# 32 products of zeros on TensorE around the first sums and transposes of a gated recurrence with a mixture of adapters

## The chip, the cores and the metric

The kernel runs on one core of one Trainium2 chip. The metric is the device time of one execution in microseconds, and the kernel before was timed in three runs. A profile of one execution by the hardware profiler goes with it. All times below that carry a place in the execution count from the start of the profile's span.

## The reference

Two steps follow each other. The first is a gated linear recurrence over 768 time steps, for each of 4 batches and 8 heads with a head size of 48:

```python
for t in range(S):
    state = alpha[:, :, t, :, None] * state + np.einsum('bhd,bhe->bhde', k[:, :, t], v[:, :, t])
    y[:, :, t] = np.einsum('bhd,bhde->bhe', q[:, :, t], state)
```

The result, laid out as 3072 rows of 384, goes through a mixture of adapters: each row chooses two of eight adapters by the largest of `x @ w_gate`, weighs them with a softmax over the two, and adds `w * (x @ A[e]) @ B[e]` (rank 16) to itself:

```python
w = np.exp(sel)
w /= w.sum(-1, keepdims=True) + 1e-09
delta[mask] += w[mask, k, None] * (z @ B[e])
return (x + delta).astype(np.float32)
```

Inputs and output are float32: 19 MB to read, 4.7 MB to write.

## The kernel before

**Units.** The work is cut into 24 units: 4 batches of 6 chunks of 128 time steps, with all 8 heads of a chunk in one unit. Within a chunk the recurrence is written as products; from chunk to chunk a state of 48x48 per head is carried. For unit u the steps are:

- `ln` (ScalarE): logarithm of alpha, for one or two units at a time.
- `cum` (TensorE, L249 to L253): sums of the logarithms over the time steps of the chunk, one product with a triangular matrix, one small one with the identity and four of two columns.
- `exp` (ScalarE): the exponential of the sums and of their negative.
- `ka`, `kg` (GpSimd, L265): k and q times these, into `kgq`. In some units k and q go in two instructions (`ka` then `kg`), in the others in one (`kg`).
- `tr` (TensorE, L285) and `kq` (ScalarE): eight 128x128 transposes into a bank of PSUM, and its copy to SBUF (`kt`).
- `at` (TensorE, L298): eight products, of keys with queries, into `at_t`. This tile takes up two banks and exists once.
- `msk` (VectorE, L302): `at_t` times a triangular mask, to SBUF. `at` of the next unit waits for it, as it writes the same tile.
- `vb` (GpSimd, L279), `kv` (TensorE), `st` (VectorE, L308): cast of v, the state's update, and its scaling.
- `av` (TensorE) and `ysb` (ScalarE): the unit's output, copied into `o_t`.
- `xb` (GpSimd, L347, half of the units), `xt` (TensorE, L356), `xs` (ScalarE): the output transposed for the adapters.

For groups of up to three units the adapters follow: `z` (products with the adapters and the gate together), `gm`, `df`, `ge`, `gx`, `wu`, `dn`, `w` (choice and weights, VectorE, one exponential on ScalarE), `zw`, `zt`, `zs` (weighting and transposing). Then for each unit `dl` (TensorE, L450) and `o` (VectorE, L457) add the adapters' part, and `out` stores the unit.

**Order.** Nothing is scheduled by a planner. One list, `ORDER`, gives every step in the order in which it is issued: `cum.7.4` is step `cum` of unit 7 into bank 4 of the five free banks `M_t`. Each engine executes its own instructions in this order, and waits for the semaphores of what it needs. `Sa.12.6` in the list is a load: queue S (SP) or A (ScalarE), tensor a, k, q or v, first unit, number of units. So a load from ScalarE is issued when ScalarE's program comes to it, behind its activations. Weights have the letter w.

**Loads.** Eight loads stand ahead of everything: alpha and q of batch 0, part of the weights and alpha of batch 1 from SP, k of batch 0 and the rest of the weights from ScalarE. The others follow inside the list. Each of the four inputs has two buffers, for even and odd batches. Written out by names with the first unit of the batch, the order in which their bytes come is: a0, k0, q0, v0, weights, a6, k6, q6, v6, a12, k12, q12, v12, a18, k18, q18, v18. All stores wait for the last of these.

**Around the change.** The first steps on TensorE are `cum.0` and `cum.1`, then `cum.2`, `cum.5` and `cum.3`, then `tr.0`, whose first four transposes need only k and whose last four need q, then `cum.4`, `tr.1` and `at.0`. Constants are set ahead of the list: VectorE clears padding in `lg` (L179) and `kgq` (L187), GpSimd builds the triangular matrix and the identity.

Of the kernel before, what the change touches and what calls it, by code (L numbers as in the profile page):

```python
# [39 lines left out]
ORDER = """  # L40
Sa.0.6 Aw.3.0 Sq.0.6 Aw.2.0 Sw.0.0 Ak.0.6 Sw.1.0 Sa.6.6 ln.0 Sq.6.6 ln.1 cum.0.0 cum.1.1 ln.4 exp.0 ln.2 exp.1
cum.2.2 Sa.12.6 ka.0 cum.5.3 Av.0.6 cum.3.4 exp.2 ka.1 exp.3 ka.2 kg.0 kg.1 tr.0.0 cum.4.1 kq.0 ka.3 tr.1.2 exp.5
at.0 kg.2 kq.1 msk.0 exp.4 kg.3 tr.2.4 cw.0 at.1 kg.4 msk.1 tr.3.0 Ak.6.6 kq.2 vb.0 kq.3 at.2 vb.1 kv.0 ka.4 av.0.3
st.1 ysb.0 msk.2 kv.1 vb.2 av.1.2 xb.0 tr.4.1 ysb.1 kg.5 st.2 at.3 xt.0.4 msk.3 ln.8 av.2.0 ka.5 Sq.12.6 kv.2 ln.6
st.3 vb.5 tr.5.3 xs.0 vb.4 ysb.2 cum.6.2 kq.4 cum.7.4 vb.3 kq.5 xb.2 at.4 exp.6 kv.3 msk.4 xt.2.0 xt.1.1 exp.7 ka.6
cum.9.3 st.4 cum.8.2 Av.6.6 xs.2 at.5 ln.10 ka.7 kv.4 msk.5 xs.1 Sa.18.6 exp.8 z.0.4 av.3.0 kg.6 exp.9 gm.0 av.4.1
st.5 ysb.3 kg.7 tr.6.2 ge.0 ysb.4 df.0 gx.0 av.5.3 kq.6 wu.0 kg.8 xt.3.0 dn.0 ysb.5 w.0 tr.7.1 xs.3 zw.0 at.6 kq.7
xt.5.2 msk.6 cum.11.3 xb.4 xs.5 zt.0.0 kg.9 xt.4.4 cum.10.1 xs.4 at.7 Ak.12.6 exp.10 tr.8.2 msk.7 z.1.4 zs.0 kq.8
vb.6 tr.9.1 gm.1 vb.7 exp.11 kv.6 at.8 kg.10 df.1 st.7 gx.1 av.6.0 msk.8 ln.12 av.7.2 kv.7 kq.9 cum.12.3 vb.8 st.8
ysb.6 dl.0.1 at.9 kg.11 ge.1 ysb.7 o.0 tr.10.0 ln.14 msk.9 av.8.2 kq.10 dl.2.1 kv.8 ysb.8 vb.9 dl.1.0 o.2 Sq.18.6  # L50
at.10 exp.12 vb.11 wu.1 cum.13.2 st.9 xt.7.1 xb.8 exp.13 dn.1 o.1 kv.9 xb.6 w.1 tr.11.3 Av.12.6 vb.10 xs.7 zw.1
cum.14.0 kq.11 ka.12 xt.8.2 msk.10 xt.6.1 zt.1.4 xs.8 cum.15.3 xs.6 zs.1 av.9.2 ka.13 exp.14 st.10 dl.3.1 z.2.4 o.3
ysb.9 kg.12 at.11 ln.16 gm.2 kv.10 msk.11 dl.4.0 kg.14 exp.15 tr.12.2 xt.9.1 kq.12 df.2 av.10.3 st.11 xs.9 cum.16.2
ge.2 o.4 gx.2 ysb.10 at.12 kg.13 wu.2 exp.16 tr.14.1 msk.12 dl.5.0 xb.10 kq.14 tr.13.3 kg.15 av.11.2 dn.2 o.5 kq.13
cum.17.1 w.2 Ak.18.6 xt.10.0 ysb.11 at.13 zw.2 xs.10 xt.11.3 msk.13 vb.12 tr.15.2 xs.11 vb.13 kv.12 exp.17 z.3.0
kg.16 st.13 at.14 ln.18 gm.3 av.13.4 msk.14 zt.2.3 kq.15 kv.13 cum.18.1 kg.17 zs.2 ysb.13 av.12.2 df.3 ge.3 st.14
at.15 ysb.12 tr.16.3 msk.15 exp.18 dl.7.4 vb.14 gx.3 tr.17.2 kq.16 wu.3 vb.15 o.7 kv.14 ln.20 vb.16 av.14.1 dn.3
st.15 xb.12 at.16 ysb.14 w.3 cum.19.3 vb.17 msk.16 kq.17 av.15.4 xb.14 Av.18.6 out.2 xt.13.1 exp.19 ka.18 out.7
kv.15 zw.3 xt.14.2 xs.13 at.17 st.16 xs.14 ka.19 xt.12.3 ysb.15 msk.17 zt.3.0 dl.6.1 xs.12 cum.20.2 ln.22 z.4.4
kg.18 o.6 zs.3 dl.8.3 exp.20 kv.16 gm.4 kg.19 tr.18.0 o.8 xt.15.1 kq.18 df.4 st.17 out.8 kg.20 dl.9.2 cum.21.3 xs.15  # L60
out.3 o.9 dl.10.0 gx.4 at.18 exp.21 out.5 o.10 tr.19.1 ge.4 msk.18 out.10 cum.22.2 kq.19 kg.21 av.17.0 out.6 exp.22
dl.11.3 av.16.1 wu.4 o.11 at.19 ysb.17 out.0 dn.4 tr.20.2 msk.19 ysb.16 out.9 vb.18 tr.21.3 kq.20 out.11 xb.16 kv.18
out.4 xt.17.0 kq.21 vb.19 w.4 st.19 at.20 out.1 vb.20 xs.17 xt.16.1 zw.4 cum.23.2 kg.22 xs.16 kv.19 msk.20 exp.23
z.5.3 st.20 at.21 kg.23 gm.5 av.18.0 tr.22.4 msk.21 ysb.18 kv.20 kq.22 av.20.1 ge.5 vb.21 df.5 at.22 st.21 gx.5
ysb.20 av.19.2 vb.22 wu.5 msk.22 zt.4.0 xb.18 ysb.19 kv.21 vb.23 tr.23.4 zs.4 dn.5 xb.20 dl.14.1 st.22 xt.19.2 kq.23
w.5 kv.22 xs.19 o.14 at.23 zw.5 xt.18.0 out.14 xt.20.4 msk.23 av.22.2 xs.18 xs.20 dl.12.1 z.6.3 ysb.22 o.12 xb.22
av.21.0 zt.5.4 gm.6 ysb.21 xt.22.2 dl.13.1 st.23 zs.5 xt.21.0 xs.22 df.6 ge.6 o.13 gx.6 dl.15.4 dl.17.2 xs.21 wu.6
o.15 av.23.1 z.7.0 dn.6 o.17 out.15 ysb.23 dl.16.4 out.13 gm.7 xt.23.2 w.6 out.17 df.7 ge.7 zw.6 gx.7 xs.23 wu.7
o.16 z.8.3 zt.6.2 gm.8 dn.7 out.16 zs.6 df.8 w.7 gx.8 out.12 dl.19.4 wu.8 dl.18.2 zw.7 o.18 zt.7.0 o.19 zs.7 dl.20.2
out.18 dl.21.0 w.8 o.20 dl.22.4 out.19 zw.8 out.20 o.21 zt.8.2 o.22 zs.8 out.21 dl.23 out.22 o.23 out.23  # L70
"""


# [18 lines left out]
def kernel(  # L92
# [43 lines left out]
    def act(*args, **kw):  # L136
        recent[:] = [nc.scalar.activation(*args, **kw)]  # L137
# [11 lines left out]
    def load(ring, x, u, n, *name):  # L149
        eng = dict(S=nc.sync, A=nc.scalar)[ring]  # L150
        if x == "w":
            eng.dma_start(out=WSRC[u][0], in_=WSRC[u][1])
            return
        b, c = _place(u)
        if n == NCH:
            dma = eng.dma_start(out=home(x, b)[:, :, 0:D],  # L156
                                in_=SRC[x][b].rearrange("h (c j) d -> j (h c) d", j=C))
# [82 lines left out]
    def ln(u):  # L240
        i, _ = lof[u]
        n = len(LNS[i])
        b, c = _place(u)
        act(lgs[i % KEEP["lg"]][:, 0:n, :, 0:D],
            chunks(home("a", b))[:, c:c + n, :, 0:D], AF.Ln)

    def cum(u):
# [1 line left out]
        nc.tensor.matmul(r[:, 0:DM], suf[:, :], t[:, :, 0:D], start=True, stop=True)  # L249
        nc.tensor.matmul(r[:, DM:DM + 2 * NP], ident[:, :], off.rearrange("p a b -> p (a b)"),  # L250
                         start=True, stop=False, skip_group_check=True)
        for p in range(NP):
            nc.tensor.matmul(r[:, DM + 2 * p:DM + 2 * p + 2], pair(t, p), ones[:, :],  # L253
                             start=False, stop=(p == NP - 1), skip_group_check=True)
# [257 lines left out]
```

## Time and profile before

| | |
|---|---|
| median of 3 runs | 95.35 us (94.91 to 95.42) |
| the profiled execution itself | 95.33 us |
| its span, first to last instruction | 93.4 us |
| TensorE products, busy | 69.4 us (74%), 1088 |
| VectorE, busy | 62.8 us (67%), 165 |
| ScalarE, busy | 64.9 us (70%), 164 |
| GpSimd, busy | 62.6 us (67%), 82 |
| loads and stores | 24.17 MB, mean 259 GB/s |

In the profile PE is TensorE with its products, PEld its loading of weights, DVE is VectorE, ACT ScalarE, POOL GpSimd and SP SyncE; a q behind a name (ACTq) is the engine's queue, which issues loads. A line of a timeline gives start and length in us, engine, line of the code, operation, output and inputs, shape and count; in brackets stands how long the engine had been idle before and what ended the wait. The chain of waits gives start, length and the piece of work. A line of the busy times by stretches gives the stretch, its length, for each of PE, PEld, DVE, ACT and POOL the busy time (and the number of instructions), then the granted clock of TensorE, the busy share of the DMA engines and GB/s. Products on TensorE are pipelined: one of 128 columns is listed with its whole length, though the next starts before it ends.

### The profile page before, as it was taken

How to read it: one execution, taken by the hardware profiler on the slowest of the kernel's cores; microseconds unless marked ns; L12 is line 12 of the kernel's file. 1: busy time of each engine (PE TensorE's matmuls, PEld its weight loads, DVE VectorE, ACT ScalarE, POOL GpSimd, SP SyncE). 2: the span in 40 equal slices, each digit the busy share in tenths (PEclk: the TensorE clock that was granted, in tenths of full speed). 3: DMA queues.
4: the chain of work that ended last, by engine and by line, in shares of the span. 5: the costliest groups of instructions: out<-in, count | busy, mean ns of one | idle time of the engine just before them, and what ended most of it. 6: DMA issues, size and time to landing. Idle time of an engine off the chain costs nothing.

```text
span 93.4 us, 2795 instructions
## 1 busy us (share of the span) xinstructions
PE 69.4 (74%) x1088; PEld 54.7 (59%) x1088; DVE 62.8 (67%) x165; ACT 64.9 (70%) x164; POOL 62.6 (67%) x82
## 2 busy tenths in 40 slices
PE   0004080988899999959999998999999989994510
PEld 0002050756778697847788886887687878861100
DVE  5000000054954969796999999799999999999920
ACT  5004990794389999769999966999899666744120
POOL 6000087999793899998769999987999994200000
PEclk9999999999999999999999999999999999999965
DMA  1999999999999599999989999999817791216681
GB/s 18 292 315 317 316 316 316 301 316 303 316 313 269 163 307 305 291 310 313 307 223 316 313 294 303 305 307 286 253 68 278 263 381 51 84 49 252 259 305 66
DMA packets 29645, 24.17 MB, mean 259 GB/s; under 512 B 1856, under 2 KB 29632, under 8 KB 29632
## 3 DMA queue, kind: packets, MB, share of 16 engines
q1 hardware_dynamic: 16928, 14.35, 49.6%
q10 hardware_dynamic: 12704, 9.65, 36.3%
q8 instruction: 8, 0.13, 0.6%
q14 instruction: 5, 0.04, 0.2%
HBM read 19.28 MB, written 4.72 MB: 257 GB/s over the span
## 4 chain that ended last, share of the span: by engine, by line
DMA 32%; DVE 25%; PE 14%; ACT 12%; POOL 5%; issue 5%; SPq 2%; ACTq 2%; DVEq 0%; POOLq 0%
DMA a_t<-in_alpha_dram 18%; DMA kq_t<-in_q_dram 14%; DVE am L302 11%; DVE o_t L457 5%; POOL kgq L265 4%; ACT ex L137 4%; PE M_t L285 3%; PE at_t L298 3%; DVE sb L308 3%; ACT o_t L140 2%; DVE zw L433 2%; ACT kt L140 2%; SPq L156 2%; ACTq L156 2%; PE M_t L450 1%
## 5 line engine op out<-in xcount | busy, mean ns | idle before, releaser
L265 POOL TENSOR_TENSOR kgq<-kq_t,ex 128x384 bf16<-128x384 f32 (+1 forms) x36 | 45.0, 1274 | 12.9 <-DMA kq_t<-in_k_dram 9.7
L302 DVE TENSOR_TENSOR am<-at_t,mask 128x1024 bf16<-128x1024 f32 x24 | 29.3, 1219 | 20.7 <-PE at_t L298 20.6
L137 ACT ACTIVATE ex<-M_t 128x392 f32<-128x392 f32 (+1 forms) x48 | 21.6, 534 | 0.6 <-PE at_t L298 0.5
L285 PE MATMUL M_t<-ident,kgq 128*128 128x128 bf16 x192 | 17.3, 238 | 2.8 <-POOL kgq L265 2.7
L140 ACT COPY kt<-M_t 128x512 f32<-128x512 f32 x24 | 14.7, 615 | 4.5 <-PE M_t L285 3.9
L249 PE MATMUL M_t<-lg,suf 128*128 128x384 bf16 x24 | 8.6, 366 | 12.1 <-ACT lg L137 12.1
L140 ACT COPY o_t<-M_t 128x384 f32<-128x384 f32 x25 | 12.4, 520 | 5.7 <-PE M_t L339 5.0
L137 ACT ACTIVATE lg<-a_t 128x768 bf16<-128x768 f32 (+1 forms) x13 | 10.5, 824 | 7.9 <-DMA a_t<-in_alpha_dram 7.1
L285 PEld LDWEIGHTS <-kgq 128*128 128x128 bf16 x192 | 12.8, 105 | 5.0 <-POOL kgq L265 3.4
L457 DVE TENSOR_TENSOR o_t<-M_t,o_t 128x384 f32<-128x384 f32 x23 | 12.4, 549 | 1.2 <-PE M_t L450 1.1
L308 DVE TENSOR_TENSOR sb<-S_t,ex 128x384 bf16<-128x384 f32 x20 | 11.0, 549 | 1.7 <-PE S_t L322 1.7
L279 POOL CAST vb<-v_t 128x384 bf16<-128x384 f32 x24 | 11.6, 506 | 0.0
L298 PE MATMUL at_t<-kt 48*128 48x128 bf16 x192 | 10.4, 233 | 1.3 <-DVE am L302 0.9
L339 PE MATMUL M_t<-vb,am 128*128 128x48 bf16 x192 | 9.2, 188 | 0.0
L347 POOL CAST xb<-o_t 128x384 bf16<-128x384 f32 x12 | 6.0, 505 | 4.6 <-ACT o_t L140 4.6
L250 PEld LDWEIGHTS <-ident 128*128 128x128 bf16 x24 | 2.4, 101 | 11.1 <-issue 10.8
L298 PEld LDWEIGHTS <-kt 48*128 48x128 bf16 x192 | 6.3, 99 | 4.0 <-issue 2.1
L450 PE MATMUL M_t<-B_all,zs 128*128 128x384 bf16 x24 | 7.3, 327 | 1.0 <-ACT zs L140 0.8
L339 PEld LDWEIGHTS <-am 128*128 128x128 bf16 x192 | 7.5, 100 | 0.3
L322 PE MATMUL S_t<-vb,kgq 128*128 128x96 bf16 x80 | 7.1, 216 | 0.0
L332 PE MATMUL M_t<-sb,kt 128*128 128x96 bf16 x80 | 7.1, 213 | 0.1
L356 PE MATMUL M_t<-ident,o_t 128*128 128x128 f32 x36 | 7.0, 303 | 0.2 <-DVE o_t L457 0.2
(53 smaller groups left out, 101.6 us busy)
## 6 DMA issues: line engine op xcount, KB each, us to landing
out_dram<-o_t SPq DMA_DIRECT2D x24, 192.0 KB, 2.3
B_st<-in_moe_B_dram ACTq DMA_DIRECT2D x1, 192.0 KB, 2.7
W_st<-in_moe_A_dram SPq DMA_DIRECT2D x2, 96.0 KB, 9.4
a_t<-in_alpha_dram SPq DMA_DIRECT2D x4, 0.2 KB, 12.9
kq_t<-in_q_dram SPq DMA_DIRECT2D x4, 0.2 KB, 16.6
kq_t<-in_k_dram ACTq DMA_DIRECT2D x4, 0.2 KB, 8.7
v_t<-in_v_dram ACTq DMA_DIRECT2D x4, 0.2 KB, 7.5
G_st<-in_moe_w_gate_dram ACTq DMA_DIRECT2D x1, 12.0 KB, 5.5
```

The lines of the kernel that those rows point to most:

```text
L137: recent[:] = [nc.scalar.activation(*args, **kw)]
L140: recent[:] = [nc.scalar.copy(*args)]
L249: nc.tensor.matmul(r[:, 0:DM], suf[:, :], t[:, :, 0:D], start=True, stop=True)
L265: nc.gpsimd.tensor_tensor(out=kgq[u % KEEP["kg"]][:, part, :, 0:D], in0=kq_t[b % 2].rearrange("p w (h c) d -> p w c h d", c=NCH)[:, part, ...
L279: nc.gpsimd.tensor_copy(out=vbt[u % KEEP["vb"]], in_=chunks(home("v", b))[:, c, :, 0:D])
L285: nc.tensor.transpose(t[:, w, p, :], pair(kgq[u % KEEP["kg"]][:, w], p), ident[:, :])
L298: nc.tensor.matmul(at_t[:, hh, p, :], kq[rows, 0, p, :], kq[rows, 1, p, :], start=True, stop=True)
L302: nc.vector.tensor_tensor(out=am[u % KEEP["am"]].rearrange("p a b t -> p (a b) t"), in0=at_t.rearrange("p a b t -> p (a b) t"), in1=_bc_mi ...
L308: nc.vector.tensor_tensor(out=sb[u % KEEP["sb"]].rearrange("p a b d -> p (a b) d"), in0=S_t.rearrange("p a b d -> p (a b) d"), in1=_bc(ex[ ...
L339: nc.tensor.matmul(y[:, h * D:(h + 1) * D], am[u % KEEP["am"]][:, hh, p, :], vbt[u % KEEP["vb"]][:, h, :], start=(c == 0 and h == 0), stop ...
L450: nc.tensor.matmul(bank("av" if hold else "dl", u)[:, 0:DM], zst[g % KEEP["zs"]].bitcast(F2)[:, j * P:(j + 1) * P], B_all[:, :], start=not ...
L457: nc.vector.tensor_tensor(out=o_t[u], in0=bank("dl", u)[:, 0:DM], in1=o_t[u], op=ALU.add)
```

## The change

A tile of 128x512 zeros in bfloat16 is set on VectorE ahead of the other constants. A new step `busy.N` issues N products of a 128x128 part of it with all 512 columns of it, into the first half of `at_t`. Nothing reads these results; the first `at` writes the tile anew, on the same engine. Four such steps stand in the list, with 13, 10, 7 and 2 products: ahead of `cum.0`, between `cum.1` and `cum.2`, between `cum.3` and `tr.0`, and between `tr.1` and `at.0`. The rest of the list has the same steps in the same order, with its lines broken in other places; the steps of the gates and the unit that is kept in PSUM (`HOLD`) are the same in both kernels.

```diff
 ORDER = """
-Sa.0.6 Aw.3.0 Sq.0.6 Aw.2.0 Sw.0.0 Ak.0.6 Sw.1.0 Sa.6.6 ln.0 Sq.6.6 ln.1 cum.0.0 cum.1.1 ln.4 exp.0 ln.2 exp.1
-cum.2.2 Sa.12.6 ka.0 cum.5.3 Av.0.6 cum.3.4 exp.2 ka.1 exp.3 ka.2 kg.0 kg.1 tr.0.0 cum.4.1 kq.0 ka.3 tr.1.2 exp.5
-at.0 kg.2 kq.1 msk.0 exp.4 kg.3 tr.2.4 cw.0 at.1 kg.4 msk.1 tr.3.0 Ak.6.6 kq.2 vb.0 kq.3 at.2 vb.1 kv.0 ka.4 av.0.3
+Sa.0.6 Aw.3.0 Sq.0.6 Aw.2.0 Sw.0.0 Ak.0.6 Sw.1.0 Sa.6.6 ln.0 Sq.6.6 ln.1 busy.13 cum.0.0 cum.1.1 ln.4 exp.0 ln.2 exp.1
+busy.10 cum.2.2 Sa.12.6 ka.0 cum.5.3 Av.0.6 cum.3.4 exp.2 ka.1 exp.3 ka.2 kg.0 kg.1 busy.7 tr.0.0 cum.4.1 kq.0 ka.3
+tr.1.2 exp.5 busy.2 at.0 kg.2 kq.1 msk.0 exp.4 kg.3 tr.2.4 cw.0 at.1 kg.4 msk.1 tr.3.0 Ak.6.6 kq.2 vb.0 kq.3 at.2 vb.1
...
+    zero = consts.tile([P, 512], F2, name="zero")
+    nc.vector.memset(zero, 0.0)
     suf = consts.tile([P, P], F2, name="suf")
...
+    def busy(n):
+
+        for _ in range(n):
+            nc.tensor.matmul(at_t[:, 0].rearrange("p a s -> p (a s)"), zero[:, 0:P], zero[:, :],
+                             start=True, stop=True)
+
...
-               w=w, zw=zw, zt=zt, zs=zs, dl=dl, o=o, out=store, cw=cw)
+               w=w, zw=zw, zt=zt, zs=zs, dl=dl, o=o, out=store, cw=cw, busy=busy)
```

More of the change, by code (lines that the diff above doesn't have):

```diff
@@ L40 @@
 ORDER = """
-Sa.0.6 Aw.3.0 Sq.0.6 Aw.2.0 Sw.0.0 Ak.0.6 Sw.1.0 Sa.6.6 ln.0 Sq.6.6 ln.1 cum.0.0 cum.1.1 ln.4 exp.0 ln.2 exp.1
-cum.2.2 Sa.12.6 ka.0 cum.5.3 Av.0.6 cum.3.4 exp.2 ka.1 exp.3 ka.2 kg.0 kg.1 tr.0.0 cum.4.1 kq.0 ka.3 tr.1.2 exp.5
-at.0 kg.2 kq.1 msk.0 exp.4 kg.3 tr.2.4 cw.0 at.1 kg.4 msk.1 tr.3.0 Ak.6.6 kq.2 vb.0 kq.3 at.2 vb.1 kv.0 ka.4 av.0.3
-st.1 ysb.0 msk.2 kv.1 vb.2 av.1.2 xb.0 tr.4.1 ysb.1 kg.5 st.2 at.3 xt.0.4 msk.3 ln.8 av.2.0 ka.5 Sq.12.6 kv.2 ln.6
-st.3 vb.5 tr.5.3 xs.0 vb.4 ysb.2 cum.6.2 kq.4 cum.7.4 vb.3 kq.5 xb.2 at.4 exp.6 kv.3 msk.4 xt.2.0 xt.1.1 exp.7 ka.6
@@ L46 @@
[L46 to L55, printed above, removed]
@@ L56 @@
-kg.16 st.13 at.14 ln.18 gm.3 av.13.4 msk.14 zt.2.3 kq.15 kv.13 cum.18.1 kg.17 zs.2 ysb.13 av.12.2 df.3 ge.3 st.14
[L57 to L70, printed above, removed]
+Sa.0.6 Aw.3.0 Sq.0.6 Aw.2.0 Sw.0.0 Ak.0.6 Sw.1.0 Sa.6.6 ln.0 Sq.6.6 ln.1 busy.13 cum.0.0 cum.1.1 ln.4 exp.0 ln.2 exp.1
@@ new lines @@
+busy.10 cum.2.2 Sa.12.6 ka.0 cum.5.3 Av.0.6 cum.3.4 exp.2 ka.1 exp.3 ka.2 kg.0 kg.1 busy.7 tr.0.0 cum.4.1 kq.0 ka.3
+tr.1.2 exp.5 busy.2 at.0 kg.2 kq.1 msk.0 exp.4 kg.3 tr.2.4 cw.0 at.1 kg.4 msk.1 tr.3.0 Ak.6.6 kq.2 vb.0 kq.3 at.2 vb.1
+kv.0 ka.4 av.0.3 st.1 ysb.0 msk.2 kv.1 vb.2 av.1.2 xb.0 tr.4.1 ysb.1 kg.5 st.2 at.3 xt.0.4 msk.3 ln.8 av.2.0 ka.5
+Sq.12.6 kv.2 ln.6 st.3 vb.5 tr.5.3 xs.0 vb.4 ysb.2 cum.6.2 kq.4 cum.7.4 vb.3 kq.5 xb.2 at.4 exp.6 kv.3 msk.4 xt.2.0
+xt.1.1 exp.7 ka.6 cum.9.3 st.4 cum.8.2 Av.6.6 xs.2 at.5 ln.10 ka.7 kv.4 msk.5 xs.1 Sa.18.6 exp.8 z.0.4 av.3.0 kg.6
@@ new lines @@
+exp.9 gm.0 av.4.1 st.5 ysb.3 kg.7 tr.6.2 ge.0 ysb.4 df.0 gx.0 av.5.3 kq.6 wu.0 kg.8 xt.3.0 dn.0 ysb.5 w.0 tr.7.1 xs.3
+zw.0 at.6 kq.7 xt.5.2 msk.6 cum.11.3 xb.4 xs.5 zt.0.0 kg.9 xt.4.4 cum.10.1 xs.4 at.7 Ak.12.6 exp.10 tr.8.2 msk.7 z.1.4
+zs.0 kq.8 vb.6 tr.9.1 gm.1 vb.7 exp.11 kv.6 at.8 kg.10 df.1 st.7 gx.1 av.6.0 msk.8 ln.12 av.7.2 kv.7 kq.9 cum.12.3
+vb.8 st.8 ysb.6 dl.0.1 at.9 kg.11 ge.1 ysb.7 o.0 tr.10.0 ln.14 msk.9 av.8.2 kq.10 dl.2.1 kv.8 ysb.8 vb.9 dl.1.0 o.2
+Sq.18.6 at.10 exp.12 vb.11 wu.1 cum.13.2 st.9 xt.7.1 xb.8 exp.13 dn.1 o.1 kv.9 xb.6 w.1 tr.11.3 Av.12.6 vb.10 xs.7
@@ new lines @@
+zw.1 cum.14.0 kq.11 ka.12 xt.8.2 msk.10 xt.6.1 zt.1.4 xs.8 cum.15.3 xs.6 zs.1 av.9.2 ka.13 exp.14 st.10 dl.3.1 z.2.4
+o.3 ysb.9 kg.12 at.11 ln.16 gm.2 kv.10 msk.11 dl.4.0 kg.14 exp.15 tr.12.2 xt.9.1 kq.12 df.2 av.10.3 st.11 xs.9
+cum.16.2 ge.2 o.4 gx.2 ysb.10 at.12 kg.13 wu.2 exp.16 tr.14.1 msk.12 dl.5.0 xb.10 kq.14 tr.13.3 kg.15 av.11.2 dn.2 o.5
+kq.13 cum.17.1 w.2 Ak.18.6 xt.10.0 ysb.11 at.13 zw.2 xs.10 xt.11.3 msk.13 vb.12 tr.15.2 xs.11 vb.13 kv.12 exp.17 z.3.0
+kg.16 st.13 at.14 ln.18 gm.3 av.13.4 msk.14 zt.2.3 kq.15 kv.13 cum.18.1 kg.17 zs.2 ysb.13 av.12.2 df.3 ge.3 st.14
@@ new lines @@
+at.15 ysb.12 tr.16.3 msk.15 exp.18 dl.7.4 vb.14 gx.3 tr.17.2 kq.16 wu.3 vb.15 o.7 kv.14 ln.20 vb.16 av.14.1 dn.3 st.15
+xb.12 at.16 ysb.14 w.3 cum.19.3 vb.17 msk.16 kq.17 av.15.4 xb.14 Av.18.6 out.2 xt.13.1 exp.19 ka.18 out.7 kv.15 zw.3
+xt.14.2 xs.13 at.17 st.16 xs.14 ka.19 xt.12.3 ysb.15 msk.17 zt.3.0 dl.6.1 xs.12 cum.20.2 ln.22 z.4.4 kg.18 o.6 zs.3
+dl.8.3 exp.20 kv.16 gm.4 kg.19 tr.18.0 o.8 xt.15.1 kq.18 df.4 st.17 out.8 kg.20 dl.9.2 cum.21.3 xs.15 out.3 o.9
+dl.10.0 gx.4 at.18 exp.21 out.5 o.10 tr.19.1 ge.4 msk.18 out.10 cum.22.2 kq.19 kg.21 av.17.0 out.6 exp.22 dl.11.3
@@ new lines @@
+av.16.1 wu.4 o.11 at.19 ysb.17 out.0 dn.4 tr.20.2 msk.19 ysb.16 out.9 vb.18 tr.21.3 kq.20 out.11 xb.16 kv.18 out.4
+xt.17.0 kq.21 vb.19 w.4 st.19 at.20 out.1 vb.20 xs.17 xt.16.1 zw.4 cum.23.2 kg.22 xs.16 kv.19 msk.20 exp.23 z.5.3
+st.20 at.21 kg.23 gm.5 av.18.0 tr.22.4 msk.21 ysb.18 kv.20 kq.22 av.20.1 ge.5 vb.21 df.5 at.22 st.21 gx.5 ysb.20
+av.19.2 vb.22 wu.5 msk.22 zt.4.0 xb.18 ysb.19 kv.21 vb.23 tr.23.4 zs.4 dn.5 xb.20 dl.14.1 st.22 xt.19.2 kq.23 w.5
+kv.22 xs.19 o.14 at.23 zw.5 xt.18.0 out.14 xt.20.4 msk.23 av.22.2 xs.18 xs.20 dl.12.1 z.6.3 ysb.22 o.12 xb.22 av.21.0
@@ L71 @@
+zt.5.4 gm.6 ysb.21 xt.22.2 dl.13.1 st.23 zs.5 xt.21.0 xs.22 df.6 ge.6 o.13 gx.6 dl.15.4 dl.17.2 xs.21 wu.6 o.15
+av.23.1 z.7.0 dn.6 o.17 out.15 ysb.23 dl.16.4 out.13 gm.7 xt.23.2 w.6 out.17 df.7 ge.7 zw.6 gx.7 xs.23 wu.7 o.16 z.8.3
+zt.6.2 gm.8 dn.7 out.16 zs.6 df.8 w.7 gx.8 out.12 dl.19.4 wu.8 dl.18.2 zw.7 o.18 zt.7.0 o.19 zs.7 dl.20.2 out.18
+dl.21.0 w.8 o.20 dl.22.4 out.19 zw.8 out.20 o.21 zt.8.2 o.22 zs.8 out.21 dl.23 out.22 o.23 out.23
 """
```

## The prediction

> **What bounds the kernel now.** I read the chain of waits first, cut to 14 to 32 us: who ended last, piece by piece.
>
> ```profile
> 15.32 1.00 POOL kgq L265
> 16.37 0.61 PE M_t L285 x4
> 17.41 0.88 PE M_t L285 x8
> 18.28 0.56 PE at_t L298 x8
> 18.94 1.24 DVE am L302
> ...
> 29.08 0.18 PE M_t L249
> 29.27 0.01 PE M_t L250
> 29.27 0.11 PE M_t L253 x4
> 29.38 0.01 issue
> 29.39 0.05 ACT ex L137
> 29.44 0.03 issue
> 29.47 0.70 ACTq L156
> ```
>
> From the arrival of the first q (GpSimd starts on it at 15.32) TensorE is on the path again and again, and the stretch ends at 29.47 with ScalarE issuing a load: v of the second batch (Av.6). The PE pieces of that stretch add up to 9.6 us, 8.4 of them before 28.2.
>
> Second, the timeline of TensorE. These are the same eight transposes before and after 28 us:
>
> ```profile
> 17.27 1.01 PE L285 MATMUL M_t<-ident,kgq 128*128 128x128 bf16 x8
> 28.21 0.61 PE L285 MATMUL M_t<-ident,kgq 128*128 128x128 bf16 x8
> ```
>
> By line and form one takes 308 ns before 28 us and 220 after. Start to start that is (1.01-0.31)/7 = 0.10 and (0.61-0.22)/7 = 0.056 us; another early group (1.10 for eight) gives 0.113, so about 0.107. TensorE runs at half rate until 28.1 us. The page's granted-clock row shows nothing of this: it reads full speed from the start, and I go by the durations.
>
> Third, busy time by stretches, for the load queue, and the GpSimd timeline for who waits for loads.
>
> ```profile
> 26.00:30.00 4.00, 4.00 (x64) 3.19 (x63) 2.04 (x3) 3.60 (x9) 2.39 (x6) 1.00 1.06 306
> 29.60:32.20 2.60, 2.60 (x43) 1.99 (x39) 2.26 (x3) 2.60 (x8) 1.96 (x2) 1.00 0.52 137
> 38.60:40.40 1.80, 1.79 (x40) 1.52 (x38) 1.74 (x7) 1.68 (x6) 1.80 (x3) 1.00 1.02 278
> 46.40:48.80 2.40, 2.40 (x48) 2.09 (x46) 2.37 (x5) 2.37 (x9) 1.79 (x2) 1.00 0.85 224
> ```
>
> The last column is GB/s. Loads run at about 316 when one is queued behind another. At 29.6 the second batch's q is nearly in, Av.6 is issued only at 29.47, and its bytes come about 1.5 us later (34 GB/s over 30.2 to 31.0, 165 over 31.0 to 32.0). Lost: 2.6 x (1-137/316) = 1.47 us; by the same sum 0.22 at 38.6 and 0.70 at 46.4.
>
> ```profile
> 32.24 3.74 POOL L265 TENSOR_TENSOR kgq<-kq_t,ex 128x384 bf16<-128x384 f32 x3 [0.31 <-DMA kq_t<-in_q_dram]
> 49.05 3.75 POOL L265 TENSOR_TENSOR kgq<-kq_t,ex 128x384 bf16<-128x384 f32 x3 [0.86 <-PE M_t L377]
> 64.98 5.54 POOL L265 TENSOR_TENSOR kgq<-kq_t,ex 128x384 bf16<-128x384 f32 x4 [0.47 <-DMA kq_t<-in_q_dram]
> ```
>
> This is the row that decides. Each batch starts when its q lands: 15.3, 32.2, 49.0, 65.0 us. (The second wait is put down to PE, but L377 there is no input of kg.12; in the order of the code it is q.) From 64.98 to the end is 28.4 us, in which the timeline of VectorE shows no gap from 67.04 to 83. TensorE is long at full rate there, so the end can move only as the fourth q moves.
>
> **What the Trainium skill says.** "TensorE: Matmul & The Clock Gate", Part 1, "What's actually happening": the array runs at half clock by default and is released after about 3.4 us of sustained activity, in a window that doesn't start with the kernel; an idle window takes it back. The trace agrees: half rate through the gapped work up to 24 us, full rate at 28.1 after TensorE has been without a gap since 23.91. "Wait — 56ns, not 53.3ns?" on the same page: start to start 106.7 and 426.7 ns at 128 and 512 columns cold, 55.6 and 215.7 warm; the trace's 0.107 and 0.056 are those for 128. "DMA: Bandwidth & Descriptors", "Issuing engines are not separate DMA queues": loads from SP and ScalarE share the same 16 engines; the trace has one rate of 316 GB/s whichever issues.
>
> **The change, part by part.** No row shows a 512-column product. Four times the trace's 128-column pitch gives 0.43 us at half rate and 0.22 at full; I keep both ends. That zeros count as activity no run here shows; I assume it, with the alternative as a rival.
>
> The zero fill: L179 clears two tiles of 128x128 words in 0.30 us, so 128x256 words is about 0.3 on VectorE, at 0.9 to 1.2 us. The memsets behind it end 0.3 later, at 2.6; nothing reads them before the first sum at 8.24. Cost 0.
>
> busy.13, from 1.2 us: 13 x 0.43 = 5.6, done by 6.8 even at half rate. TensorE would wait for ln.0 until 8.24. Cost 0.
>
> busy.10, behind cum.1 (about 9.2): 2.2 us at full rate, to 11.4, ahead of cum.2 at 11.77: cost 0. At half rate 4.3, to 13.5: cum.2, and behind it exp.2 and ka.2, 1.7 late; of that GpSimd's wait for q at 15.32 (0.5 idle) and the spare before ka.2 (13.8) leave about 0.4 to 0.7.
>
> busy.7, behind cum.3 (13.1): 1.6 or 3.0 us. tr.0's second half waits for q until 16.37: cost 0, unless both groups are cold.
>
> busy.2, between tr.1 and at.0: nothing hides it, 0.44 (0.86 cold). Against it, with tr.0 to tr.1 at full rate, tr.1 ends about 17.7, when kg.1 is there, so at.0 starts at about 18.15 instead of 18.21. Even.
>
> What a full clock then saves: at.0 to at.4 end 0.2 sooner each (0.61 to 0.40), and TensorE's pieces up to 28.2 go from 8.4 to some 4.5 us. GpSimd takes over as the limit: it is solid to 23.40, loses its waits of 0.68 and 0.53 for ysb, and ends kg.5 and ka.5 near 25.85 instead of 26.5. tr.5 can follow at 25.9 instead of 28.21, and kq.5, cum.6 and cum.7 bring Av.6 to about 27.2, 2.3 earlier. Queued by 27.9 (29.4 less 1.5) it leaves no hole: a12, the next alpha, ends 1.4 us sooner.
>
> Now what is late next. The next k (Ak.12, at 37.08) doesn't follow. On ScalarE it stands behind xs.4, that behind xt.4 on TensorE (36.60), that behind xb.4 on GpSimd (35.92 to 36.42), which follows 3.74 us of kg.6 to kg.8, started by the landing of q6 at 32.2. q6 was issued at 15.71 and isn't touched by the change. So Ak.12 moves at most 0.2 (xt.4 no longer behind zt.0), and the hole opens there: k12 is issued 0.3 before a12 runs out, as Av.6 was 0.1 before, so about 1.3 is lost where 0.22 was. Net 1.4 - 1.1 = 0.3 at k12 and q12. Av.12 (45.68) hangs on a12 (ScalarE waited 0.83 for it at 41.11): up to 1.2 earlier, so 0.6 of the 0.70 hole at 46.4 comes back. Ak.18 (53.35) hangs on q12 again (49.05 + 3.75 on GpSimd + 0.45 of tr.13 = 53.25) and moves 0.3, so about 0.4 is lost again. The fourth q: 0.3 + 0.6 - 0.4 = 0.5 earlier, and with it the end: span 92.9, and the profiled execution's own 95.33 becomes 94.8. That execution stands on the median of the runs (95.35).
>
> **Rivals.** Whole hole gained: if q12 does move with a12, by 1.4, the end follows: 93.9. For it: ScalarE is ahead by 2 us at 29. Against: the GpSimd row at 32.24.
>
> Nothing gained: the hole only moves from 30 to 38 and the one at 46 stays, because cum.13 is held by VectorE: 95.2 to 95.35. For it: loads pace every batch.
>
> Slower, by one mechanism: the clock isn't full when at.0 comes. TensorE is idle from about 14.9 to 16.4 even with the products; if the clock falls back there, or zeros never raised it, busy.2 costs 0.86 in front of at.0, all behind it runs as now, Av.6 goes out at 30.3, the hole grows by 0.86: 96.2. With all products cold, at.0 is 2.7 late: 98. It decides once Av.6 is later than 29.47. For it: 17.9 to 21.3 was 89% busy and didn't raise the clock. This is also the case in which the change doesn't do what it is built to do.
>
> **How the numbers follow.** My forecast has 0.40 (own range 94.3 to 95.0), the whole hole 0.14, nothing 0.25, slower 0.21. Some 0.5%, 0.48 us, is what a measurement here can tell from no change. Faster: 0.33 of the forecast's and 0.14: 0.47. Slower: 0.18 of its 0.21. Within: the rest, 0.35. The range leaves out a tenth each side: 93.8 to 96.2.
>
> **What would show it.** L285's eight at 17 us in 0.61 instead of 1.01; Av.6 issued near 27.2 and no hole at 30; a new one near 37.5; Ak.12 still near 36.9; GpSimd's waits for q ending at 32.2, 48.7 and 64.4. Wrong if the half-rate durations remain at 17 us, if q6 lands at another time (its last packets now share engines with v's), or if Ak.12 moves by more than 0.5.

## The result and the profile after

| | before | after |
|---|---|---|
| median of the first comparison, 20 runs each | 95.50 us | 95.11 us |
| the profiled execution, its span | 95.33, 93.4 us | 94.46, 92.5 us |
| q of the fourth batch, last packet lands | 64.91 us | 64.19 us |
| from there to the end of the span | 28.4 us | 28.3 us |

The ratio after to before is 0.990, 95% interval 0.9864 to 0.9937: faster, by 0.6 to 1.4%. The forecast was 94.8, the range 93.8 to 96.2. Run again beside the last experiments, the same kernel gave 0.9938 (0.9906 to 0.997), medians 94.58 and 95.16. Single executions of one kernel lie up to 5 us apart (94.63 to 99.54 before, 93.57 to 97.76 after), and a ratio is formed from the undisturbed ones alone, for the changed kernel 9 of 20, so that it need not be the quotient of the medians beside it (here 0.996).

**The clock.** Busy time by stretches, core 0, columns as before (stretch, length, PE, PEld, DVE, ACT, POOL, granted clock, DMA share, GB/s):

```profile
3.66:7.07 3.41, 3.32 (x8) 1.06 (x7) 0.00 (x0) 0.00 (x0) 0.00 (x0) 1.00 1.05 305
7.07:10.48 3.41, 1.97 (x18) 1.09 (x18) 0.00 (x0) 1.96 (x5) 0.00 (x0) 1.00 1.09 317
...
13.89:17.30 3.41, 1.09 (x12) 0.65 (x10) 0.00 (x0) 0.21 (x1) 2.75 (x4) 1.00 1.08 316
17.30:20.72 3.42, 3.42 (x33) 2.19 (x30) 0.70 (x1) 3.24 (x10) 3.42 (x5) 0.50 1.13 304
20.72:24.13 3.41, 1.97 (x38) 1.54 (x37) 2.08 (x3) 1.70 (x5) 3.24 (x5) 1.00 1.06 305
24.13:27.55 3.42, 3.14 (x37) 2.58 (x37) 2.09 (x4) 1.94 (x4) 3.08 (x5) 0.50 1.08 314
```

The record puts the clock at a half from 17.30 to 20.72 and from 24.13 to 27.55. The edges lie 3.41 us apart, and each fits what TensorE did in the stretch ahead of it: TensorE was busy for 3.32 of 3.41 us before 7.07 (with zeros alone), and what follows runs at full rate; it was busy for 1.09 before 17.30, and the clock fell. So zeros do raise it. But the third group ends at 14.4, the transposes of k behind it at 14.6, and q is on TensorE only at 16.9. The clock falls at the end of the stretch that holds this gap of 2.3 us, just before it is wanted. The timeline of TensorE shows the same in durations:

```profile
1.25 5.73 PE L252 MATMUL at_t<-zero 128*128 128x512 bf16 x13 [1.25 <-DVE zero L172]
...
9.21 2.32 PE L252 MATMUL at_t<-zero 128*128 128x512 bf16 x10
...
12.71 1.67 PE L252 MATMUL at_t<-zero 128*128 128x512 bf16 x7
...
17.50 1.01 PE L293 MATMUL M_t<-ident,kgq 128*128 128x128 bf16 x8
...
21.63 0.62 PE L293 MATMUL M_t<-ident,kgq 128*128 128x128 bf16 x8
...
28.21 0.61 PE L293 MATMUL M_t<-ident,kgq 128*128 128x128 bf16 x8
```

The eight transposes (L285 before, L293 now) that took 1.01 us before still take 1.01. A group inside the full-rate stretch takes 0.62 (at 21.63), one at 25.67 takes 1.03 again, and 0.61 is the rule only from 28 us on. In the chain of waits the last group stands bare on the path, and Av.6 is issued when it was before (29.47):

```profile
17.63 0.88 PE M_t L293 x8
18.51 0.85 PE at_t L252 x2
19.36 0.56 PE at_t L306 x8
...
29.48 0.70 ACTq L156
```

The first `at` is 1.1 us later than before (19.36 against 18.28). By 28.4 us the chain is level with that of before (eight transposes at 28.38, before at 28.37): it caught up in the full-rate stretch from 20.72 and after the rise at 27.55, 0.6 ahead of the rise at 28.15 before.

**The holes in the loads**, with the stretches of before, and one more:

```profile
29.60:32.20 2.60, 2.60 (x43) 1.99 (x39) 2.25 (x3) 2.60 (x7) 1.96 (x2) 1.00 0.63 168
38.60:40.40 1.80, 1.78 (x38) 1.52 (x36) 1.74 (x7) 1.80 (x7) 1.80 (x3) 1.00 0.93 241
46.40:48.80 2.40, 2.40 (x46) 1.87 (x44) 2.40 (x7) 2.40 (x8) 1.83 (x3) 1.00 1.05 282
54.60:57.00 2.40, 2.40 (x48) 2.15 (x48) 2.22 (x6) 1.68 (x4) 2.40 (x4) 1.00 0.88 232
```

Against 137, 278, 224 and 291 GB/s before: the first hole stays, the second deepens, the third closes, the fourth opens. GpSimd's starts on the second to fourth q:

```profile
32.38 3.75 POOL L273 TENSOR_TENSOR kgq<-kq_t,ex 128x384 bf16<-128x384 f32 x3 [0.40 <-DMA kq_t<-in_q_dram]
48.74 3.75 POOL L273 TENSOR_TENSOR kgq<-kq_t,ex 128x384 bf16<-128x384 f32 x3 [0.57 <-DMA kq_t<-in_q_dram]
64.25 5.52 POOL L273 TENSOR_TENSOR kgq<-kq_t,ex 128x384 bf16<-128x384 f32 x4 [0.44 <-DMA kq_t<-in_q_dram]
```

0.14 later, 0.31 earlier, 0.73 earlier. The span is 0.9 shorter, so nearly all of the gain is in the landing of the fourth q. The first place found where the two executions part for good is ScalarE's wait for the third alpha. Timeline of ScalarE, before:

```profile
41.11 0.84 ACT L137 ACTIVATE lg<-a_t 128x768 bf16<-128x768 f32 x1 [0.83 <-DMA a_t<-in_alpha_dram]
45.68 0.71 ACTq L156 DMA_DIRECT2D v_t<-in_v_dram  x1
```

and after:

```profile
40.16 0.90 ACT L137 ACTIVATE lg<-a_t 128x768 bf16<-128x768 f32 x1
44.78 0.71 ACTq L156 DMA_DIRECT2D v_t<-in_v_dram  x1
```

The wait is gone, so Av.12 goes out 0.9 earlier, and the hole at 46 closes. This alpha lands earlier although v in front of it was issued no earlier. The trace gives each of these loads sixteen completions, as many as there are DMA engines, and they are read here as one per engine: before they came from 39.0 to 41.09, after from 39.1 to 39.93. The fastest engine is where it was; the slowest is 1.2 us sooner. Before, ScalarE's wait ended at 41.11, with the last of the sixteen.

### The profile page after: what moved, and what is told of

Its sections match the earlier page's. It is cut to its first block, busy times and chain, and to the rows that moved or that the text cites. A ratio compares the mean times of both kernels' runs of the same rounds, so it can differ in the third digit from the quotient of the medians.

```text
span 92.5 us, 2860 instructions
## 1 busy us (share of the span) xinstructions
PE 76.8 (83%) x1120; PEld 56.5 (61%) x1120; DVE 63.1 (68%) x166; ACT 64.7 (70%) x164; POOL 62.6 (68%) x82
## 4 chain that ended last, share of the span: by engine, by line
DMA 34%; DVE 26%; PE 14%; ACT 13%; issue 5%; ACTq 2%; SPq 1%; POOL 1%; DVEq 0%
DMA a_t<-in_alpha_dram 19%; DMA kq_t<-in_q_dram 15%; DVE am L310 11%; DVE o_t L465 5%; ACT ex L137 4%; PE M_t L293 3%; DVE sb L316 3%; ACT xs L140 3%; PE at_t L306 3%; ACT o_t L140 2%; DVE zw L441 2%; ACTq L156 1%; SPq L156 1%; ACT kt L140 1%; ACT zs L140 1%
## 5 line engine op out<-in xcount | busy, mean ns | idle before, releaser
L293 PE MATMUL M_t<-ident,kgq 128*128 128x128 bf16 x192 | 16.6, 231 | 2.9 <-POOL kgq L273 2.8
L293 PEld LDWEIGHTS <-kgq 128*128 128x128 bf16 x192 | 12.2, 103 | 5.3 <-POOL kgq L273 3.8
L252 PE MATMUL at_t<-zero 128*128 128x512 bf16 x32 | 10.8, 497 | 1.3 <-DVE zero L172 1.3
L257 PE MATMUL M_t<-lg,suf 128*128 128x384 bf16 x24 | 7.7, 327 | 1.9 <-ACT lg L137 1.8
L252 PEld LDWEIGHTS <-zero 128*128 128x128 bf16 x32 | 3.6, 120 | 5.8 <-issue 3.0
```

Of the source, the lines that this page charges most:

```text
L252: nc.tensor.matmul(at_t[:, 0].rearrange("p a s -> p (a s)"), zero[:, 0:P], zero[:, :], start=True, stop=True)
L293: nc.tensor.transpose(t[:, w, p, :], pair(kgq[u % KEEP["kg"]][:, w], p), ident[:, :])
```

## The experiments

All kernels here compute the whole reference; they add or remove products of zeros, or move loads in the list. Lines of the list are cut to the words around an edit. Two questions were asked. Is the gain the clock? And what sets the landing of the fourth q?

**A third group that spans the wait for q (e1_bridge).** After, with one number changed:

```diff
-kg.0 kg.1 busy.7 tr.0.0 cum.4.1 kq.0 ka.3
+kg.0 kg.1 busy.16 tr.0.0 cum.4.1 kq.0 ka.3
```

> The kernel after with 16 products instead of 7 in the third group, so that TensorE is busy until about 16.3 us, when q lands, and the clock should no longer fall back at 17.3. Theory A (loads pace the batches; an earlier TensorE helps only through the issue of Av.6 and what hangs on it): Av.6 near 27.3 instead of 29.5, the hole at 30 us gone, Ak.12 still near 37.0, and the end at most 0.5 us sooner than the kernel after: ratio to the kernel before 0.985 to 0.992. Theory B (the end follows TensorE's early chain): 1.5 to 2 us sooner than the kernel after, ratio 0.970 to 0.977.

Ratio 0.9868 (0.9817 to 0.9919), median 94.26, profiled 94.33 with span 92.4. The clock is at full rate from 3.9 to 85.8 us. Its chain of waits:

```profile
18.58 0.43 PE at_t L252 x2
19.01 0.35 PE at_t L306 x8
...
27.96 0.69 ACTq L156
```

The last group costs the 0.43 of the forecast instead of 0.85, and Av.6 goes out at 27.96. The hole at 30 is gone (312 GB/s from 29 to 33), and Ak.12 goes out at 36.49, 0.6 earlier than before and not quite where it was expected. With the clock where it was meant to be, the kernel gains 1.3%, 0.3 points more than the change as it is and 0.7 more than in its repetition, and the intervals overlap. A full clock is no large lever here.

**One load at a time, on the kernel before (e2_v6early, e3_kearly).** First v of the second batch alone, ahead of what TensorE holds up:

```diff
-kv.2 ln.6 st.3 vb.5
+kv.2 ln.6 Av.6.6 st.3 vb.5
...
-cum.9.3 st.4 cum.8.2 Av.6.6 xs.2
+cum.9.3 st.4 cum.8.2 xs.2
```

> The kernel before, no products, with the load Av.6 moved up in ScalarE's order to right behind ln.6, so that it is issued near 26 instead of 29.47 while TensorE stays at half rate. Theory A: the hole at 30 us (1.47 us of full rate) closes, but k12 is issued no sooner, so that 0.3 to 0.6 us reach the end: ratio 0.994 to 0.997. A's rival (the whole hole is worth its size): ratio 0.985. Theory B: nothing, 1.000.

Ratio 1.0104 (1.0049 to 1.016): slower, a miss. The profiled execution (95.12, span 93.1) shows the hole go from one place to the next (busy time by stretches; the rates before are 202 and 295):

```profile
29.00:33.00 4.00, 3.78 (x66) 2.97 (x64) 2.92 (x4) 3.87 (x10) 2.67 (x3) 1.00 1.08 316
37.00:41.00 4.00, 3.77 (x77) 3.27 (x75) 3.45 (x8) 3.37 (x11) 4.00 (x5) 1.00 0.67 192
```

Alpha 12 lands 1.5 us sooner, at 39.54, but its chain of waits has k of the third batch go out only behind TensorE's and ScalarE's work on the q that landed at 32.2:

```profile
36.99 0.18 PE M_t L356 x3
...
37.26 0.02 ACT kq_t L156
...
37.31 9.85 DMA kq_t<-in_k_dram
```

That is the loop of the forecast: q, GpSimd, `xb.4`, `xt.4`, `xs.4`, then the next k. Why most executions of this kernel are slower than before stays unexplained: the profiled one, at 95.12, is not.

Then both late loads of k alone, each moved up behind the copy `kq` of the batch before:

```diff
-av.5.3 kq.6 wu.0
+av.5.3 kq.6 Ak.12.6 wu.0
...
-xs.4 at.7 Ak.12.6 exp.10
+xs.4 at.7 exp.10
...
-xt.9.1 kq.12 df.2
+xt.9.1 kq.12 Ak.18.6 df.2
...
-cum.17.1 w.2 Ak.18.6 xt.10.0
+cum.17.1 w.2 xt.10.0
```

> The kernel before, no products, with Ak.12 moved up to behind kq.6 and Ak.18 to behind kq.12 (2 to 2.7 us sooner on ScalarE); Av.6 stays where it is. Theory A: only the small losses at 38.6 and 54.6 go (0.22 and 0.19), so 0.2 to 0.4 us: ratio 0.996 to 0.998. Theory B: 1.000.

Ratio 0.9939 (0.9905 to 0.9974), median 95.19. Somewhat more than the expected gain; but three of 14 executions took about 105 us, at a mean granted clock of 0.90 where the others have 0.96 to 0.98. None of the three was profiled, and the cause is open.

**All four late loads, without any zeros (e4_all_before).** The edits of the two runs above, and Av.12 from behind `tr.11` to behind `ln.14`:

```diff
-tr.10.0 ln.14 msk.9
+tr.10.0 ln.14 Av.12.6 msk.9
...
-w.1 tr.11.3 Av.12.6 vb.10
+w.1 tr.11.3 vb.10
```

> The kernel before, no products, with all four late loads moved up: Av.6 behind ln.6, Ak.12 behind kq.6, Av.12 behind ln.14, Ak.18 behind kq.12. Theory A: the holes together are 2.6 us of full rate (1.47 + 0.22 + 0.70 + 0.19), the fourth q lands up to 2.5 sooner, and VectorE, which has little idle time after 44 us, lets through 1 to 2 of it: ratio 0.979 to 0.990, more than e2 and e3 together. Theory B: nothing, 1.000, since TensorE's early chain is as it was.

Ratio 0.9791 (0.9741 to 0.9841), median 93.30, span 91.1: twice the gain of the change, with TensorE at half rate to 28 us as before. All four holes are closed (busy time by stretches):

```profile
29.00:33.00 4.00, 3.77 (x67) 2.95 (x65) 3.10 (x4) 4.00 (x11) 3.11 (x4) 1.00 1.08 316
37.00:41.00 4.00, 3.76 (x77) 3.28 (x75) 3.47 (x8) 3.79 (x11) 4.00 (x5) 1.00 1.08 314
46.00:49.00 3.00, 3.00 (x57) 2.47 (x55) 3.00 (x8) 3.00 (x9) 2.73 (x4) 1.00 1.08 314
54.00:58.00 4.00, 4.00 (x82) 3.37 (x79) 3.94 (x10) 3.81 (x10) 4.00 (x4) 1.00 1.08 316
```

The fourth q lands at 62.45, 2.46 us earlier; the span is 2.3 shorter. Loads that wait for compute set the time, and not TensorE's rate.

**Zeros that are too short to raise the clock (e5_short).** After, with products of 16 columns in place of 512; the same number of instructions, a thirty-second of the columns (the first group takes 0.51 us instead of 5.73):

```diff
-            nc.tensor.matmul(at_t[:, 0].rearrange("p a s -> p (a s)"), zero[:, 0:P], zero[:, :],
+            nc.tensor.matmul(at_t[:, 0].rearrange("p a s -> p (a s)")[:, 0:16], zero[:, 0:P], zero[:, 0:16],
```

> The kernel after with the same 32 products in the same places, but 16 columns wide instead of 512, so that they take next to no time and should not raise the clock. If the change works through the clock alone: half rate to about 28 us as before the change, and the time of the kernel before, ratio 0.997 to 1.003. If something else in the change (the shifted constants, the other code) did it: the ratio of the kernel after, 0.99.

Ratio 0.9912 (0.9874 to 0.995). The profiled execution took 94.82, span 92.3. Its timeline of TensorE shows the half rate, that of GpSimd the fourth q 0.87 earlier than before:

```profile
17.41 1.01 PE L293 MATMUL M_t<-ident,kgq 128*128 128x128 bf16 x8
```

```profile
64.11 1.97 POOL L273 TENSOR_TENSOR kgq<-kq_t,ex 128x384 bf16<-128x384 f32 x2 [0.27 <-DMA kq_t<-in_q_dram]
```

So a gain of this size can be had with a cold clock. It isn't as steady: the 22 executions fall into two groups, 9 between 93.75 and 94.8, of which the ratio speaks, and 13 from 95.5 up, and the median of all is 96.00 (before: 95.24).

**Without the last group (e6_nobusy2).**

```diff
-tr.1.2 exp.5 busy.2 at.0 kg.2
+tr.1.2 exp.5 at.0 kg.2
```

> The kernel after without the last group of two products, which stood on the path in front of at.0 for 0.85 us at half rate. Theory A: at.0 starts 0.4 to 0.9 sooner, but Av.6 is issued within 0.7 us of where it was, and the loads behind it hang on q6: ratio 0.986 to 0.993, as the kernel after within 0.3%. Theory B: 0.4 to 0.9 us below the kernel after, ratio 0.981 to 0.986.

Ratio 0.9907 (0.9867 to 0.9947), median 94.15, the same as after within the intervals, as Theory A had it. In its profile the clock is at a half from 17.0 to 27.3, and Av.6 goes out at 29.08, 0.4 before the changed kernel's: with 0.85 taken off the path before `at.0`, half arrives.

**All four loads, with zeros (e7_all_after, e8_all_bridge).** The changed kernel with the eight lines of load edits that e2, e3 and e4 show together, and the same with this line besides:

```diff
-kg.0 kg.1 busy.7 tr.0.0 cum.4.1 kq.0 ka.3
+kg.0 kg.1 busy.16 tr.0.0 cum.4.1 kq.0 ka.3
```

> The kernel after (13, 10, 7 and 2 products) with the four late loads moved up as in e4, whose ratio was 0.979. Av.6 no longer hangs on TensorE. Theory A: the products now find nothing to bring forward but VectorE's early work, and the clock falls back twice on the way: 0.976 to 0.980. Theory B: the gain of the kernel after adds to that of e4: 0.969.

> e7 with 16 products instead of 7 in the third group, so that the clock stays full from the first microseconds (as in e1, ratio 0.987). Theory A: VectorE enters the second batch some 1.4 us ahead of e4; at most 0.5 us of that reaches the end, as the fourth q still starts the last 28 us: 0.972 to 0.977. Theory B: both gains in full, 0.966 or less.

Ratios 0.9797 (0.9737 to 0.9857) and 0.9776 (0.9722 to 0.983), medians 93.14 and 92.86; the span of e8's profiled execution is 90.8. e7 lies where Theory A had it, e8 just outside (0.972 to 0.977). Next to e4's 0.9791 the zeros add nothing that the intervals tell apart. e8 is the fastest kernel of the study, 2.2% below before, and its six runs lie between 92.57 and 93.32. But e8 was meant to have a full clock, and in its profile the clock is at a half from 8.24 to 11.65 and again from 21.89 to 28.72; e7's has the like. So the ratios don't show what a clock that stays full would add once the loads don't wait. A hint is in the six executions of e8: two have a mean granted clock of 0.974 and 0.976, which leaves no room for a fall ahead of the last microseconds, and they took 92.57 and 92.61; the other four, at 0.92 to 0.96, took 92.78 to 93.32. By that it would be some tenths of a microsecond.

**The change again, and its instructions alone (e9_after_again, e10_short32, e11_short128).** e9 is the changed kernel. e10 is the kernel before with 32 products of 16 columns ahead of the first sum, and e11 with 128; a smaller tile of zeros is declared last, so that no other address moves:

```diff
-ln.0 Sq.6.6 ln.1 cum.0.0 cum.1.1
+ln.0 Sq.6.6 ln.1 busy.32 cum.0.0 cum.1.1
```

> The kernel after once more, on the chip of the next three, as their measure. 0.99 as before, with single runs on both sides of 95 us. In the profile the instruction fetches (16 KB each, queue q8) should fall at 22 to 23, 30, 39, 47, 54.6 and 62.5 us, between the loads of q, where the kernel before has them at 26.6, 43.5 and 59.3, inside them.

> The kernel before with 32 products of 16 columns ahead of cum.0, and the tile of zeros declared after all others, so that no other tile moves. No clock effect: half rate until about 28 us. Theory C (the change shifts when TensorE's instructions are fetched, 64 instructions ahead, so that the fetches no longer hit the loads of q that start a batch): as e5, fast runs near 94.2, ratio 0.99, q18 landing near 64.0. If the shift of the tiles' addresses in SBUF did it in e5: ratio 1.000. If the clock does it (theory A): 1.000.

> e10 with 128 such products: 256 more instructions on TensorE[...] are just one fetch of 16 KB, so that the fetches fall where the kernel before has them, one number later. Theory C: the gain of e10 goes, ratio 1.000, with fetches near 26.6, 43.5 and 59.3. If any narrow products help in another way: 0.99 or less.

e9: 0.9938 (0.9906 to 0.997), and a second profile of the same code. In it the clock's edges fall elsewhere: full from 6.39, half from 9.80 to 13.21, and full from there on. Timeline of TensorE, and chain of waits:

```profile
17.70 0.83 PE L293 MATMUL M_t<-ident,kgq 128*128 128x128 bf16 x8
```

```profile
18.52 0.43 PE at_t L252 x2
...
27.92 0.68 ACTq L156
```

and busy time by stretches:

```profile
29.00:33.00 4.00, 3.19 (x64) 2.51 (x62) 3.19 (x9) 4.00 (x11) 2.59 (x3) 1.00 1.07 309
37.00:41.00 4.00, 3.84 (x76) 3.23 (x75) 3.05 (x7) 3.45 (x11) 4.00 (x5) 1.00 0.78 216
46.00:49.00 3.00, 3.00 (x56) 2.41 (x54) 3.00 (x8) 3.00 (x10) 2.45 (x3) 1.00 1.05 293
54.00:58.00 4.00, 3.96 (x76) 3.43 (x77) 3.78 (x10) 3.52 (x9) 4.00 (x5) 1.00 0.98 279
```

Up to the fourth q (63.67) this execution is the forecast's: Av.6 at 27.92, the hole at 30 gone, a new one at 38, Ak.12 pinned at 37.11, the hole at 46 mostly closed. In all it took 95.62 us, span 93.7, more than the 95.33 before: it loses the gain again at its end, as the last section shows. The clock had fallen already at 9.80. So the second group of zeros ran at half rate, the third ended at 15.9 instead of 14.4, and TensorE then waited 1.07 us for q instead of 2.32: from 13.21 to 16.62 it was busy for 2.82 of 3.41 us, and the clock held. So what the clock does at the wait depends on where the 3.41 us stretches happen to lie, and that changes from one execution to the next.

e10: 0.9945 (0.9907 to 0.9983), with TensorE at half rate to 27.2 us. Timeline of TensorE:

```profile
2.41 1.02 PE L252 MATMUL at_t<-zero 128*128 128x16 bf16 x32 [2.41 <-DVE zero L215]
17.39 1.01 PE L293 MATMUL M_t<-ident,kgq 128*128 128x128 bf16 x8
```

Its fourth q lands at 63.67, 1.24 earlier than before, as in e9; the execution took 95.05, span 92.0. The ratio can't be told from e9's; the median of all 22 runs, 95.10, is only 0.06 below that of before, against e9's 0.58. So 64 instructions more, which compute nothing, leave the clock cold and move no address, can bring the fourth q in as early, and a gain in the total comes less often.

e11: 1.0106 (1.007 to 1.0141). The gain is gone, and more. It isn't a clean control: a transfer of instructions now falls into k of the first batch, the first q lands at 16.54 (before: 15.25), and q of the third batch comes ahead of its k. Nor are the other transfers back in their places: at 28.3, 37.3, 45.5, 53.8 and 61.7 they come 1.5 to 2.4 us behind those of before.

**Many narrow products and then seven wide ones (e12_after_thin).** Meant to keep the clock's part and undo the rest: 128 products in all (256 instructions), of which 26 are wide.

```diff
-Sq.6.6 ln.1 busy.13 cum.0.0 cum.1.1
+Sq.6.6 ln.1 thin.102 busy.7 cum.0.0 cum.1.1
```

> The kernel after with six of its first 13 wide products replaced by 102 narrow ones, 128 products in all: the clock is raised early as in the kernel after, but the fetches are back at the places of the kernel before. This gives the clock's own part. Theory A alone: 0.99, as e9. Theory C alone: 1.000. Both: 0.994 to 0.997.

Six runs, 95.23 to 98.39, median 97.63, no interval. The same two things happened as in e11 (a transfer at 7.7 us, the order of k and q turned round), so it says nothing of the clock by itself. Inconclusive.

## Why the prediction was right, and where it wasn't

The number was right (94.8 forecast, 95.11 and 94.58 measured). The step on which it rested, that a full clock issues Av.6 2.3 us earlier, failed in the first profile and came true in e9, so that the number owes something to luck. Working it out from the rates, a stretch of length T at r GB/s loses T(1 - r/316). The lost time, in us, and the landing of the fourth q in eight profiled executions:

| | 0 to 26 | hole 29-33 | hole 37-41 | hole 46-49 | hole 54-58 | the rest to 58 | sum | fourth q |
|---|---|---|---|---|---|---|---|---|
| before | 2.60 | 1.44 | 0.27 | 0.72 | 0.23 | 0.29 | 5.55 | 64.91 |
| after | 2.76 | 1.25 | 0.43 | 0.27 | 0.61 | 0.08 | 5.40 | 64.19 |
| third group of 16 (e1) | 2.91 | 0.05 | 0.66 | 0.73 | 0.27 | 0.12 | 4.73 | 63.71 |
| after again (e9) | 2.93 | 0.09 | 1.27 | 0.22 | 0.47 | 0.05 | 5.03 | 63.67 |
| short zeros, no clock (e5) | 2.72 | 1.04 | 0.28 | 1.04 | 0.23 | 0.25 | 5.56 | 64.04 |
| zeros, no clock (e10) | 2.78 | 0.91 | 0.35 | 0.23 | 0.20 | 0.12 | 4.59 | 63.67 |
| v early (e2) | 2.64 | 0.00 | 1.57 | 0.30 | 0.86 | 0.20 | 5.57 | 64.58 |
| all loads early (e4) | 2.93 | 0.00 | 0.03 | 0.02 | 0.00 | 0.26 | 3.24 | 62.45 |

What the sum doesn't give is in the last load's own spread, from its first engine's completion to its last: 1.9 us before, 1.4 after, 1.6 in e1, 1.1 in e9 and e5, 1.7 in e10, 1.6 in e2, 2.0 in e4. Lost time and spread together, against before: after -0.15 and -0.5 (the fourth q moved by -0.72), e1 -0.82 and -0.3 (-1.20), e9 -0.52 and -0.8 (-1.24), e5 0.01 and -0.8 (-0.87), e10 -0.96 and -0.2 (-1.24), e2 0.02 and -0.3 (-0.33), e4 -2.31 and +0.1 (-2.46). The account closes to 0.3 us in each. In e5 all of it is the spread.

- **Half rate until 28 us, and zeros count as activity:** right. Zeros alone brought TensorE to full rate at 7.1 us.
- **The first three groups at no cost:** right; the first sum starts when its logarithm is there, and what ends at 14.4 is ahead of q.
- **What a full clock then saves, Av.6 at 27.2:** the step that failed in the first profile. There the clock fell back over the gap from 14.6 to 16.9, the mechanism of the rival "slower"; the half-rate durations remained at 17 us, which the prediction had named as a sign of being wrong; the last group cost 0.85, and Av.6 came at 29.48. In e9 the clock held and it came at 27.92. The rival was wrong on what follows: it had all behind the first `at` run as before, but two of the next groups came into a full-rate stretch, Av.6 was not later than before, and the kernel not slower. "TensorE: Matmul & The Clock Gate" of the Trainium skill (Part 1, "What's actually happening") has the clock fall after an idle window; here a window with 1.09 of 3.41 us busy was enough, and one with 1.97 (20.72 to 24.13) as well, while another with 1.97 (7.07 to 10.48) was not. In all profiles the nine falls ahead of 30 us follow stretches with 1.09 to 2.10 us busy, and e1 went through one with 1.61 (3.92 to 7.33) at full rate, so the busy time alone doesn't decide it.
- **The hole reappears at 38, Ak.12 and Ak.18 held by q:** right. In e9 the holes at 29 to 33 and 37 to 41 go from 1.44 and 0.27 to 0.09 and 1.27; the forecast had 1.3 at the second. e2 shows the same with one load moved, and e4 what the loop was worth. In e1 it holds less well: Ak.12 moved by 0.6, and the second hole cost 0.66.
- **The hole at 46 by 0.6, that at 54 back by 0.4:** 0.5 and 0.2 in e9, 0.45 and 0.4 in the first profile; but in e1, with the clock full, the hole at 46 stayed (0.73).
- **The fourth q 0.5 earlier, the end with it:** 0.73 on GpSimd and 0.9 in the span of the profiled execution. In the median of the runs the gain was 0.4 to 0.6, and the 94.8 lay 0.3 from the first median and 0.2 from the second.
- **What the sum lacked:** a term for how evenly a load's sixteen engines finish. In the first profile the holes together lose as much as before (2.56 against 2.66), as in the rival "nothing gained". The one at 46 gives back 0.45 behind the earlier a12, and those at 38 and 54 take 0.54 more; the one at 30, from which the forecast took 1.4, gives 0.19. What is left is the slowest engine of the last q (0.5) and the stretches with a full queue (0.2 less lost, against 0.2 more ahead of 26 us). The forecast's number was right for that execution by luck, by a sum whose main term wasn't there.

**What might move the slowest engine.** Beside the loads, the trace has transfers of instructions, the larger ones (queue q8) of 16 KB in one packet, which takes about 1.0 us on one engine. By the queues' list, 26 to 30 us, before:

```profile
q1 hardware_dynamic: 1458, 1.12, 95.8%
q10 hardware_dynamic: 134, 0.09, 8.5%
q8 instruction: 1, 0.02, 1.6%
```

and after:

```profile
q1 hardware_dynamic: 1423, 1.09, 93.3%
q10 hardware_dynamic: 215, 0.15, 13.3%
```

Before they come at 26.6, 35.8, 43.5 and 52.3, in stretches with a full queue, the second of them in the bytes of a12. After they come at 30.3, 39.4, 47.0 and 54.6, in or at the holes: the 32 products and their 32 loads of weights put TensorE's program 64 instructions ahead, and e10, which adds as many of both and else only a fill of zeros, moves them in the same way. e5 and e10, with the same count, have them in the same stretches, within 0.8 us of these times. One engine late by 1.0 us is 0.06 us of the mean rate; four of them make 0.25, and the stretches with a full queue lose 0.21 less. That the place of these transfers is also what made a12 and the last q land more evenly is argued and not shown: e5 has its a12 as late as before (41.17), the last q of all of them still meets a transfer (59.3 before, 62.5 after), and e11 and e12, meant to decide it, moved other things too. How far the spread of a load varies between executions of one kernel is not known either: each kernel has one profile, the changed one two (1.4 and 1.1 us for the last q). Open as well: why e2 is slower in most runs, the 105 us of e3, and how much of the runs' median, beyond e10's, is the clock's.

## What to carry to other kernels

When the end follows a load, trace that load back to the instruction that holds up its issue, and move the issue: here four moved loads were worth 2%, while a full clock (e1) gave 0.4 to 0.8 points more than products that left it cold (e5, e10), with overlapping intervals. To keep the clock here, the zeros had to cover the wait ahead of the place where it is wanted (e1), wherever the 3.41 us stretches lie. A change of a percent needs many runs and more than one profile: two profiles of one kernel here had different clocks and different holes.
